# Last token block of an attention and MLP layer: one half of its output products made early instead of two

## The chip, the cores and the metric

The kernel runs on one core of a Trainium2 chip. The time is the device time of one execution in microseconds (us), the median of three runs. Inside the text, "at 1032.14" means 1032.14 us after the start of the profiled span, which is 1048.1 us long.

## What is computed

The reference is one transformer layer whose two branches are multiplied: self-attention with 32 heads of 32 on a normalised input, and an MLP with GELU, whose output goes through SiLU and gates the attention output. There are 2048 tokens of width 1024, in bf16.

```python
def reference(A_x, A_wqkv, A_wo, B_x, B_w1, B_b1, B_w2, B_b2):
    x  = A_x
    xn = _layernorm(x)
    s  = attention(xn, A_wqkv, A_wo)      # softmax(q k^T / sqrt(32)) v, 32 heads, then @ wo
    g  = _silu(gelu(_layernorm(xn) @ B_w1 + B_b1) @ B_w2 + B_b2)
    return x + s * g
```

The change touches only the last line of this: the product with `wo`, the multiplication by the gate `g`, and the addition of `x`.

## The kernel before: the parts that matter

The heads are worked through in 8 groups (`HG = 8`) of 4 heads, and within a group the queries in 8 blocks of 256 tokens (`qb`, `NQB = 8`). Attention of one block needs 8 "units"; each unit is one set of 8 score matmuls (TensorE, `L1176`), two exponentials of 128x1024 (ScalarE, `L1190`), and products with V and with ones (TensorE, `L730`). Everything else (projections, MLP, output products) is TensorE work that is laid between the score matmuls.

Who does what when is decided before the kernel runs, in Python. Every operation is recorded with an assumed duration, and a planner (`_Plan.run`) plays the five engines against each other and fixes for each engine one order of instructions. On the chip each engine runs its list in that order and waits on semaphores where the data demand it.

The output products come in the last head group. A `wo_item` is one 128-token half (`t2`) of a block and one 512-column half (`nh`) of the output: 8 matmuls of 128x512 that add up in one PSUM bank, one for each head group. Seven of them use head groups whose attention was finished long before; the eighth uses `ot7`, the block's attention in the last head group.

```python
def wo_item(qb, t2, nh, lo, hi):
    tb = 2 * qb + t2
    ri, xr, gr, rt = res_of(qb, t2)               # buffers with x and g of these 128 tokens
    it = _Item("wo")
    it.last = lo > 0                              # such an item opens only after the last score matmul
    for hc in range(lo, hi):
        ...                                       # bank += OT[hc]^T @ wo[hc][:, 512 columns]   (L735)
    ...
    if hi < HG:                                   # the early part: head groups 0 to 6
        dve(pk = bank * 0.5 * gr)                 # L1333, f32 result
        dve(pk = pk + xr)                         # L1335, f32
    else:
        dve(gr = bank * 0.5 * gr)                 # L1337
        if lo == 0:                               # a whole item
            dve(xr = gr + xr)                     # L1340, bf16
        else:                                     # the rest of a split item: head group 7 alone
            last = lambda e: e.tensor_tensor(xr[:, sl], gr[:, sl], pk, op=ALU.add)   # L1342
            if t2 == 0:
                pool(last, ...)                   # GpSimd
            else:
                dve(last, ...)                    # VectorE
            dma(...)                              # L1347: this 128x512 quarter goes out
    plan.queues["wo"].append(it)

# ... for each block qb of the last head group, after its attention:
lastq = qb == NQB - 1
for t2 in range(2):
    if not lastq:
        wo_load(qb, t2)
    for nh in range(2):
        wo_item(qb, t2, nh, 7 if lastq else 0, 8)
    if not lastq:
        wo_store(qb, t2)                          # L1312: 128x1024 of the output goes out
if qb == PART:                                    # PART = 4
    for t2 in range(2):
        wo_load(NQB - 1, t2)
        for nh in range(2):
            wo_item(NQB - 1, t2, nh, 0, 7)        # the early part of the last block
```

So for blocks 0 to 6 all four items of a block are whole. Block 7 is split: its four items over head groups 0 to 6 (28 matmuls) stand in the queue after those of block 4, and what is left for the very end is four single matmuls, each with its own multiplication and addition, and four quarters of the output.

Of the kernel before, what the change touches and what calls it, by code (L numbers as in the profile page):

```python
# [37 lines left out]
DN = (2, 3, 4, 5, 6, 7, 8, 9, 10, 11, 12, 13, 14, 15)  # L38
EVD = ()
PART = 4  # L40
WLAT = 3300
TR0 = 7
NCUT = 2
# [8 lines left out]
XB = 5  # L52
XW = 9
WVT = 6
ENGS = ("PE", "ACT", "DVE", "POOL", "SP")


# [18 lines left out]
class _Plan:  # L76
# [54 lines left out]
    def run(self, total_units, dense_slack):  # L131
# [51 lines left out]
        def release(o, t):  # L183
            for u in o.users:
                u.left -= 1
                f = o.fin
                if u.eng == "PE" and o.eng == "PE":
                    f = o.start + o.occ
                if f > u.ready:
                    u.ready = f  # L190
                if u.left == 0:
                    became_ready(u, t)
# [80 lines left out]
        def pe_step(t):  # L273
# [86 lines left out]
                                break  # L360
            best = None
            paced = None
            for c in cands:
                if c[0] <= t:
                    if c[1] == 0 and heads["pro"] >= len(self.queues["pro"]) and \
                            state["done"] < dense_total * (self.units_of(state["s"]) - dense_slack) / total_units:
                        paced = c
                        continue
                    if best is None or c[1] < best[1]:
                        best = c  # L370
                else:
                    nxt = min(nxt, c[0])
# [188 lines left out]
def bass_recurrent_scan__mha_block__mixer_channel_mlp__prompt_kernel(  # L561
# [39 lines left out]
    with ExitStack() as st:  # L601
# [79 lines left out]
        def c_b16(n):  # L681
            return 75 + 0.52 * n
# [632 lines left out]
        def wo_item(qb, t2, nh, lo, hi):  # L1315

            tb = 2 * qb + t2
            ri, xr, gr, rt = res_of(qb, t2)
            it = _Item("wo")
            it.need = wo_dma[qb, t2]  # L1320
            it.last = lo > 0
            for hc in range(lo, hi):
                def fn(e, b, hc=hc):
                    o7 = OTr[:, hc, tb * 128:(tb + 1) * 128] if hc < 7 else ot7[:, tb * 128:(tb + 1) * 128]
                    return full(e, bank(b), o7, wo_sb[hc][:, nh * 512:(nh + 1) * 512], hc == lo, hc == hi - 1)
                chunk(it, fn, Q512, [("OTr", hc, tb // 4) if hc < 7 else ("OT7", qb), ("wo", hc)])
            sl = slice(nh * 512, (nh + 1) * 512)
            k = 2 * t2 + nh
            pk = part[:, k]
            pt = [("h", h0 + 2 * k), ("h", h0 + 2 * k + 1)]  # L1330
            g, x = [("gr", ri, nh)], [("xr", ri, nh)]
            if hi < HG:
                dve(lambda e: e.scalar_tensor_tensor(pk, bank(it.bank), 0.5, gr[:, sl], op0=ALU.mult, op1=ALU.mult),  # L1333
                    c_ps(512), g, pt, 0, it)
                dve(lambda e: e.tensor_tensor(pk, pk, xr[:, sl], op=ALU.add), c_f32(512), x + pt, pt, 2.4)  # L1335
            else:
                dve(lambda e: e.scalar_tensor_tensor(gr[:, sl], bank(it.bank), 0.5, gr[:, sl], op0=ALU.mult, op1=ALU.mult),  # L1337
                    c_ps(512), g, g, 0, it)
                if lo == 0:
                    dve(lambda e: e.tensor_tensor(xr[:, sl], gr[:, sl], xr[:, sl], op=ALU.add), c_b16(512), g + x, x, 1)  # L1340
                else:
                    last = lambda e: e.tensor_tensor(xr[:, sl], gr[:, sl], pk, op=ALU.add)  # L1342
                    if t2 == 0:
                        pool(last, 1100, g + pt, x, 1)
                    else:
                        dve(last, c_f32(512), g + pt, x, 1)
                    dma(f"os{ri}{nh}", lambda e: e.dma_start(out2[tb * 128:(tb + 1) * 128, sl], xr[:, sl]), 131072, x, [])  # L1347
            plan.queues["wo"].append(it)
# [9 lines left out]
        for w in range(HG):  # L1358
            if w + 1 < HG:
                proj(w + 1, w)  # L1360
            else:

                def over(toks):
                    ops = []
                    for t in toks:
                        for d in [plan.last_w.get(t)] + plan.readers.get(t, []):
                            if d is not None and d not in ops:
                                ops.append(d)
                    return ops
                dead7 = over([("K", 0, n) for n in range(NPR)])  # L1370
                for qt in range(4):
                    dead = over([("xnT", t, h) for t in range(4 * qt, 4 * qt + 4) for h in range(2)])
                    for hg in range(HG - 1):
                        dma(f"otl{hg}{qt}", lambda e, hg=hg, qt=qt: e.dma_start(OTr[:, hg, qt * 512:(qt + 1) * 512],
                                                                          o_d[hg, :, qt * 512:(qt + 1) * 512]), 131072,
                            [("o_d", hg, 2 * qt), ("o_d", hg, 2 * qt + 1)], [("OTr", hg, qt)], 5, dead)
                    for hc in (2 * qt, 2 * qt + 1):
                        wd = over([[("wqk", 0)], [("wqk", 1)], [("wqk", 2)], [("wv",)], [("wv",)], [("dg", 0), ("dg", 1), ("sbc",)],
                                   [("Q", 0, n) for n in range(NPR)], [("Q", 0, n) for n in range(NPR)]][hc])
                        dma(f"wo{hc}", lambda e, hc=hc: e.dma_start(wo_sb[hc], A_wo[hc * 128:(hc + 1) * 128, :]), 262144, [],  # L1380
                            [("wo", hc)], 5, wd)
            for qb in range(NQB):
                g = w * NQB + qb
                if g == 0:

                    two = [_Item("pv"), _Item("pv")]
                    for pv in two:
                        pv.exp_of = {}
                    xs = []
                    for pos, (i, kp) in enumerate([(0, 0), (0, 1), (1, 0), (1, 1)] + [(i, kp) for kp in range(2, NKP) for i in range(2)]):  # L1390
                        x, vc = unit(i * 8 + kp, two[i], pos)
                        xs.append(x)
                        two[i].chunks.append(vc)
                    for pv in two:
                        pv.trigger = xs[TR0]
                        plan.pv_queue.append(pv)
                if g < 2:
                    norm(g, two[g], ot_t[g][:], [("ot", g)])
                    dma(f"ot{g}", lambda e, g=g, qb=qb: e.dma_start(o_d[0, :, qb * 256:(qb + 1) * 256], ot_t[g][:]),
                        65536, [("ot", g)], [("o_d", 0, qb)])  # L1400
                    continue
                pv = _Item("pv")
                pv.exp_of = {}
                vcs, ocs = [], []
                for kp in range(NKP):
                    x, vc = unit(g * 8 + kp, pv)
                    exps[g * 8 + kp] = x
                    vcs.append(vc)
                    if kp % 4 == 3:
                        ocs += ones_four(g * 8 + kp - 3, pv)  # L1410
                if len(ocs) == 3:
                    pv.chunks = vcs[0:6] + ocs[0:1] + vcs[6:7] + ocs[1:2] + vcs[7:8] + ocs[2:3]
                else:
                    pv.chunks = [vcs[0:6] + ocs[0:1] + vcs[6:8] + ocs[1:2], vcs + ocs][OLAG]
                late.append((pv, g))
                plan.pv_queue.append(pv)
                i = g % 2
                if w < HG - 1:
                    norm(g, pv, ot_t[i][:], [("ot", i)])
                    dma(f"ot{i}", lambda e, w=w, qb=qb, i=i: e.dma_start(o_d[w, :, qb * 256:(qb + 1) * 256], ot_t[i][:]),  # L1420
                        65536, [("ot", i)], [("o_d", w, qb)])
                    continue
                norm(g, pv, ot7[:, qb * 256:(qb + 1) * 256], [("OT7", qb)], dead7)

                lastq = qb == NQB - 1
                for t2 in range(2):
                    if not lastq:
                        wo_load(qb, t2)
                    for nh in range(2):
                        wo_item(qb, t2, nh, 7 if lastq else 0, 8)  # L1430
                    if not lastq:
                        wo_store(qb, t2)
                if qb == PART:

                    for t2 in range(2):
                        wo_load(NQB - 1, t2)
                        for nh in range(2):
                            wo_item(NQB - 1, t2, nh, 0, 7)
# [63 lines left out]
```

The softmax here doesn't subtract the row's maximum and nothing guards it: scores larger than these inputs give would overflow.

## Time and profile before

| what | value |
|---|---|
| time, median of 3 runs | 1049.85 us (1048.47 to 1050.28) |
| profiled span | 1048.1 us |
| TensorE busy | 1024.4 us, 98% of the span |
| ScalarE busy | 1016.8 us, 97% |
| VectorE busy | 959.5 us, 92% |
| GpSimd busy | 14.8 us, 1% |
| DMA | 159.63 MB, mean 152 GB/s |
| granted TensorE clock in the profiled run | 0.999 |

Three of the engines are over 90% busy, so the page as a whole does not tell what a change at the end is worth. The last twenty microseconds have to be read by themselves, instruction by instruction: when the last exponential ends, when the last matmul of TensorE starts, what VectorE and GpSimd still have to do after it, and when the last transfers leave. The timeline gives these; in it "PE" is TensorE, "DVE" VectorE, "ACT" ScalarE, "POOL" GpSimd, and "SPq" the queue that issues transfers. In a row that stands for several instructions (xN) the duration runs from the start of the first to the end of the last.

### The profile page before, as it was taken

How to read it: one execution, taken by the hardware profiler on the slowest of the kernel's cores; microseconds unless marked ns; L12 is line 12 of the kernel's file. 1: busy time of each engine (PE TensorE's matmuls, PEld its weight loads, DVE VectorE, ACT ScalarE, POOL GpSimd, SP SyncE). 2: the span in 40 equal slices, each digit the busy share in tenths (PEclk: the TensorE clock that was granted, in tenths of full speed). 3: DMA queues.
4: the chain of work that ended last, by engine and by line, in shares of the span. 5: the costliest groups of instructions: out<-in, count | busy, mean ns of one | idle time of the engine just before them, and what ended most of it. 6: DMA issues, size and time to landing. Idle time of an engine off the chain costs nothing.

```text
span 1048.1 us, 32171 instructions
## 1 busy us (share of the span) xinstructions
PE 1024.4 (98%) x14338; PEld 637.1 (61%) x14338; DVE 959.5 (92%) x1452; ACT 1016.8 (97%) x1110; POOL 14.8 (1%) x28
## 2 busy tenths in 40 slices
PE   8999999999999999999999999999999999999997
PEld 5555566656666656656776566556665567664442
DVE  8579999999999989999999989999989999979897
ACT  6799999999999999999999999999999999999993
POOL 2200000000000000000000000000000000000000
PEclk9999999999999999999999999999999999999999
DMA  8943457534266357533465456533565687672431
GB/s 230 201 126 110 127 153 218 168 94 127 86 196 184 105 143 211 150 104 107 132 180 169 125 155 193 138 96 107 154 200 157 173 240 226 204 206 98 136 102 61
DMA packets 300259, 159.63 MB, mean 152 GB/s; under 512 B 38106, under 2 KB 291034, under 8 KB 300122
## 3 DMA queue, kind: packets, MB, share of 16 engines
q1 hardware_dynamic: 300122, 157.59, 53.5%
q8 instruction: 112, 1.84, 0.7%
q14 instruction: 25, 0.20, 0.1%
HBM read 142.35 MB, written 12.06 MB: 147 GB/s over the span
## 4 chain that ended last, share of the span: by engine, by line
ACT 83%; PE 12%; DVE 2%; DMA 2%; SPq 1%; issue 0%; DVEq 0%
ACT P L1190 77%; PE ps L735 7%; ACT ut L1051 5%; PE ps L730 2%; PE ps L1176 2%; ACT gw L1087 1%; DVE ut L906 1%; DMA hT<-in_A_x_dram 1%; DMA w2r<-in_B_w_dram 1%; DMA big<-gw 0%; SPq L749 0%; DVE gw L936 0%; DVE w1r L1337 0%; DVE V L806 0%; SPq L757 0%; DVE qk L834 0%
## 5 line engine op out<-in xcount | busy, mean ns | idle before, releaser
L1190 ACT ACTIVATE P<-ps 128x1024 bf16<-128x1024 f32 x1024 | 964.1, 1238 | 10.2 <-PE ps L1176 10.0
L1220 DVE TENSOR_TENSOR PA<-P 128x2048 bf16<-128x2048 bf16 x245 | 297.6, 1217 | 17.8 <-ACT P L1190 16.4
L735 PE MATMUL ps<-yT,w1r 128*128 128x256 bf16 x1792 | 232.7, 273 | 1.3 <-DVE nv L1273 0.7
L735 PE MATMUL ps<-w2r,hT 128*128 128x256 bf16 x1792 | 225.0, 273 | 3.2 <-DMA w2r<-in_B_w_dram 1.3
L735 PEld LDWEIGHTS ps<-yT,w1r 128*128 128x128 bf16 x1792 | 162.7, 98 | 57.3 <-issue 30.6
L735 PEld LDWEIGHTS ps<-w2r,hT 128*128 128x128 bf16 x1792 | 163.8, 98 | 52.2 <-issue 29.8
L730 PE MATMUL ps<-P,V 128*32 128x256 bf16 x4096 | 144.2, 274 | 1.2 <-DVE xb L1036 0.7
L1225 DVE TENSOR_TENSOR PA<-PA 128x1024 bf16<-128x1024 bf16 x201 | 135.4, 681 | 1.2
L735 PE MATMUL ps<-big,qk 128*128 128x512 bf16 (+2 forms) x568 | 132.8, 360 | 2.4 <-DMA big<-gw 0.9
L735 PE MATMUL ps<-qk,big 128*128 128x256 bf16 (+1 forms) x736 | 127.5, 306 | 0.4 <-ACT big L885 0.3
L730 PEld LDWEIGHTS ps<-P,V 128*32 128x32 bf16 x4096 | 97.2, 96 | 33.6 <-issue 22.8
L1176 PE MATMUL ps<-qk 32*128 32x256 bf16 x2048 | 107.9, 273 | 4.9 <-ACT P L1190 4.5
L1176 PE MATMUL ps<-QKT 32*128 32x256 bf16 x2048 | 101.7, 273 | 1.2 <-ACT P L1190 1.1
L735 PEld LDWEIGHTS ps<-qk,big 128*128 128x128 bf16 x736 | 64.5, 98 | 43.9 <-issue 19.4
L1036 DVE TENSOR_TENSOR xb<-ps,b1T 128x512 bf16<-128x512 f32 x112 | 76.4, 683 | 8.4 <-PE ps L735 7.1
L735 PEld LDWEIGHTS ps<-big,qk 128*128 128x128 bf16 x568 | 47.9, 98 | 53.0 <-issue 16.7
L1176 PEld LDWEIGHTS ps<-qk 32*128 32x128 bf16 x2048 | 32.1, 92 | 74.0 <-ACT P L1190 69.2
L1176 PEld LDWEIGHTS ps<-QKT 32*128 32x128 bf16 x2048 | 30.3, 92 | 70.5 <-ACT P L1190 67.2
L1051 ACT ACTIVATE ut<-ut 128x1024 f32<-128x1024 f32 x56 | 71.8, 1282 | 0.0
L1054 DVE SCALAR_TENSOR_TENSOR hT<-ut,xb 128x1024 bf16<-128x1024 f32 x56 | 67.8, 1211 | 1.3 <-ACT ut L1051 0.9
L1049 DVE SCALAR_TENSOR_TENSOR ut<-hT,xb 128x1024 f32<-128x1024 bf16 x56 | 67.9, 1214 | 0.0
L1270 DVE STREAM_TRANSPOSE nt<-ps 128x256 f32<-128x256 f32 x64 | 28.6, 446 | 22.7 <-PE ps L730 22.6
(84 smaller groups left out, 540.6 us busy)
## 6 DMA issues: line engine op xcount, KB each, us to landing
w1r<-in_B_w_dram SPq DMA_DIRECT2D x224, 256.0 KB, 3.4
w2r<-in_B_w_dram SPq DMA_DIRECT2D x128, 448.0 KB, 4.4
qk<-in_A_wqkv_dram SPq DMA_DIRECT2D x16, 256.0 KB, 3.1
g_scratch<-gw SPq DMA_DIRECT2D x32, 128.0 KB, 2.6
o_scratch<-ot SPq DMA_DIRECT2D x56, 64.0 KB, 2.9
big<-o_scratch SPq DMA_DIRECT2D x28, 128.0 KB, 3.3
hT<-in_A_x_dram SPq DMA_DIRECT2D x10, 256.0 KB, 4.9
qk<-in_A_wqkv_dram SPq DMA_DIRECT2D x4, 512.0 KB, 4.0
```

The costliest lines, as they stand in the source:

```text
L730: ins = e.matmul(dst(j), lhsT=lhsT(j), rhs=rhs(j), start=start, stop=stop, tile_position=(0, 32 * j), skip_group_check=True)
L735: return e.matmul(dst, lhsT=lhsT, rhs=rhs, start=start, stop=stop, skip_group_check=True)
L906: dve(lambda e, t=t, c=c: e.bn_stats(stats[:, t, c, :], xst[t][:, c * 512:(c + 1) * 512]), 600, [XS(t)], [("st", t, c)], 1)
L1036: dve(lambda e: e.tensor_tensor(xb_t[i2][:, p % 2].rearrange("p (k t) -> p k t", k=2), bank(it.bank).rearrange("p (k t) -> p k t", k=2), b ...
L1049: dve(lambda e, r=r: e.scalar_tensor_tensor(ut_t[i2][:, r], h[:, r], 1.0 / GA, xb[:, r], op0=ALU.add, op1=ALU.mult), c_f32(r.stop - r.star ...
L1051: act(lambda e: e.activation(ut_t[i2][:], ut_t[i2][:], ACT.Tanh, scale=GC * GA), c_acts(1024), [("ut", i2, 0), ("ut", i2, 1)], [("ut", i2, ...
L1054: dve(lambda e, r=r: e.scalar_tensor_tensor(h[:, r], ut_t[i2][:, r], 1.0, xb[:, r], op0=ALU.add, op1=ALU.mult), c_f32(r.stop - r.start), [ ...
L1176: ins = e.matmul(bank(b0[j], kk * 256, (kk + 1) * 256), lhsT=QKT[sl][32 * j:32 * j + 32, 1, kb * 128:(kb + 1) * 128], rhs=QKT[sl][32 * j:3 ...
L1190: x = act(lambda e, h=h: e.activation(P[pi][:, 2 * h:2 * h + 2].rearrange("p j k q -> p (j k q)"), ps[:, pr[h] * 1024:(pr[h] + 1) * 1024], ...
L1220: add2.append(dve(lambda e, p0=p0, a0=a0: e.tensor_tensor(PA_all[:, a0:a0 + 2].rearrange("p u j q -> p (u j) q"), P_all[:, p0:p0 + 2, :, 0 ...
L1225: add4.append(dve(lambda e, a0=a0: e.tensor_tensor(PA[a0], PA[a0], PA[a0 + 1], op=ALU.add), c_b16(1024), [("PA", a0 + 1)], [("PA", a0)], P ...
L1270: a = dve(lambda e: e.transpose(nt_t[i][:], bank(pv.bank, 256, 512)), 368, [], [("nt", i)], 1, pv)
```

## The change

Only the first half (`t2 = 0`) of block 7 is still split. The second half is no longer made in part early: its two items run whole, 8 matmuls each, as the last ones of the queue, and each of its two 512-column quarters goes out as soon as it is added up. Its additions are then those of a whole item (two bf16 inputs) in place of those with an f32 partial sum. Two planner settings come with it: `XPE`, which is zero and so adds nothing, and `LATE`, a rule that keeps TensorE from opening other work when a score matmul has been ready for longer than the planner's 5000 ns.

```diff
+LASTP = 1
+XPE = 0
+LATE = 5000
@@ planner: release
                 if u.eng == "PE" and o.eng == "PE":
                     f = o.start + o.occ
+                elif u.eng == "PE" and o.eng == "ACT":
+                    f += XPE
@@ planner: choice of TensorE's next instruction
+            hold = INF
+            if state["s"] < len(self.s_queue):
+                o = self.s_queue[state["s"]]
+                if o.left == 0 and o.ready > t and heads["pro"] >= len(self.queues["pro"]):
+                    hold = o.ready + LATE
             for c in cands:
                 if c[0] <= t:
+                    if t + c[2].occ + (100.0 if c[2].mode != state["mode"] else 0.0) > hold:
+                        nxt = min(nxt, hold - LATE)
+                        continue
@@ wo_item
                 if lo == 0:
                     dve(lambda e: e.tensor_tensor(xr[:, sl], gr[:, sl], xr[:, sl], op=ALU.add), c_b16(512), g + x, x, 1)
+                    if qb == NQB - 1:
+                        dma(f"os{ri}{nh}", lambda e: e.dma_start(out2[tb * 128:(tb + 1) * 128, sl], xr[:, sl]), 131072, x, [])
@@ last head group
                 for t2 in range(2):
-                    if not lastq:
+                    if not (lastq and t2 < LASTP):
                         wo_load(qb, t2)
                     for nh in range(2):
-                        wo_item(qb, t2, nh, 7 if lastq else 0, 8)
+                        wo_item(qb, t2, nh, 7 if lastq and t2 < LASTP else 0, 8)
                     if not lastq:
                         wo_store(qb, t2)
-                if qb == PART:
-                    for t2 in range(2):
+                if qb == PART and LASTP:
+                    for t2 in range(LASTP):
                         wo_load(NQB - 1, t2)
                         for nh in range(2):
                             wo_item(NQB - 1, t2, nh, 0, 7)
```

## The prediction

> **What bounds the kernel now.** I read the page first: ScalarE is 97% busy, TensorE 98%. A share of 98% can belong to a limiting engine or to one that is merely fed to fit, so the second view is the ScalarE timeline near the end. One row there holds the last 31 exponentials.
>
> ```profile
> PE 1024.4 (98%) x14338; PEld 637.1 (61%) x14338; DVE 959.5 (92%) x1452; ACT 1016.8 (97%) x1110; POOL 14.8 (1%) x28
> ...
> 1003.24 28.90 ACT L1190 ACTIVATE P<-ps 128x1024 bf16<-128x1024 f32 x31
> ```
>
> The reader is to see 31 exponentials in 28.90 us without a gap: 0.93 us each, and the last ends at 1003.24 + 28.90 = 1032.14. Until then ScalarE sets the pace, and TensorE's matmuls only have to fit between its demands. Third view: the chain of waits of the last 30 us, from the last product with P on.
>
> ```profile
> 1032.27 0.55 PE ps L730 x16
> 1032.82 7.68 PE ps L735 x35
> 1040.50 0.02 issue
> 1040.52 0.69 DVE V L1337
> 1041.21 2.39 DVE w1r L1337 x4
> 1043.61 0.84 DVE V L1340
> 1044.44 0.60 DVEq L1452
> 1045.05 0.60 DVE w1r L1342
> ```
>
> After the exponentials the path is 8 us of wide output matmuls on TensorE, then 5 us of VectorE, then the last store. Fourth view: the timeline of that end.
>
> ```profile
> 1040.11 1.24 PE L735 MATMUL ps<-qk 128*128 128x512 bf16 x5
> 1040.52 0.69 DVE L1337 SCALAR_TENSOR_TENSOR V<-ps,V 128x512 bf16<-128x512 f32 x1 [0.57 <-PE ps L735]
> 1041.13 2.48 DVE L1337 SCALAR_TENSOR_TENSOR w1r<-ps,w1r 128x512 bf16<-128x512 f32 x4
> 1041.89 2.27 POOL L1342 TENSOR_TENSOR w1r<-w1r,hT 128x512 bf16<-128x512 bf16 x2 [998.16 <-DVE w1r L1337]
> ...
> 1043.52 0.92 DVE L1340 TENSOR_TENSOR V<-V 128x512 bf16<-128x512 bf16 x1
> 1044.37 1.28 DVE L1342 TENSOR_TENSOR w1r<-w1r,hT 128x512 bf16<-128x512 bf16 x2
> ...
> 1044.85 1.42 SPq L1347 DMA_DIRECT2D out_dram<-w1r  x3
> ```
>
> TensorE issues five matmuls in a row, the last of block 6 and the four singles of block 7: five results in about 1 us. VectorE then needs 5 evacuations (L1337) and three additions. It ends at 1044.37 + 1.28 = 1045.65, and the span ends 2.45 us later with the last store.
>
> **What the Trainium skill says.** (1) *SBUF — State Buffer*, "Who interferes with whom": a VectorE instruction with two SBUF inputs contends with a GpSimd instruction that reads SBUF, and the later of the two blocks fully; one with at most one SBUF input and no two-port mode does not. The trace agrees: L1337, which reads one input from PSUM, keeps a pitch of 0.60 us beside GpSimd (1041.13 to 1041.89 and on), but the L1340 addition at 1043.52 takes 0.92 us where the others of its line take 0.42; it ends 0.28 us after GpSimd's last one (1041.89 + 2.27 = 1044.16). (2) *VectorE: DVE Perf Modes*, "The perf-mode tier table": a two-tensor operation runs at double rate for bf16 in SBUF, at single rate for f32. Agrees: L1340 0.42 us, the f32 L1335 and L1342 0.68. (3) *TensorE: Matmul & The Clock Gate*, "Back-to-back issue gap": 512 columns cost about 216 ns alone and about 131 in a sustained stream of pairs. The trace has the first: rows of the timeline that begin an item's last matmul stand at 1034.93 and 1040.11, three items or 24 matmuls apart, 0.216 us each. (4) *DMA: Bandwidth & Descriptors*, "Anatomy of one DMA — SWDGE (gpsimd) path", puts the fixed cost of a transfer issued by GpSimd at about 2 us; here SyncE issues, and a 128 KB store lands in 1.7 to 2.0 us.
>
> **The change part by part.** The built order of instructions (no times in it) shows what the planner does. Setting `LASTP` to 2 in the changed file gives the old order on every engine, so `XPE` and `LATE` move nothing, and the first difference stands at TensorE instruction 14,000 of 14,324: only about the last 38 us differ. ScalarE's list is the same.
>
> *Removed early:* two items of 7 matmuls for block 7's second half: 14 x 0.216 = 3.0 us of TensorE, around 1013 to 1018, and on VectorE two L1333 and two L1335, 4 x 0.68 minus overlap, about 2.5 us. *Moved forward:* the matmuls of blocks 5 and 6 fill most of the hole. By count, the new order has 4 wide matmuls fewer before the last product with P (and 4 small ones with ones fewer, 0.1 us), and after it 43 instead of 39. So TensorE gets about 1.0 us of slack before the last exponential. ScalarE was gapless there, so I take **none** of it as gain: the last exponential stays at 1032.1.
>
> *TensorE's end:* the first of the 39 starts at 1032.76 (1040.11 minus 34 x 0.216), the last at 1040.97. With 43 the last starts at 1032.76 + 42 x 0.216 = 1041.83: **0.86 us later**.
>
> *VectorE's end:* the old order ends in a heap, the new one in an even row: block 6's last item, the two singles of block 7's first half, then the two whole items of 8. An evacuation starts 0.41 us after the item's last matmul starts (1040.11 to 1040.52), so results are ready at 1038.35, 1038.57, 1038.78, 1040.51 and 1042.24. VectorE works as follows. Three L1337 at a pitch of 0.60 to 0.65: 1038.35 to 1040.26. GpSimd's two additions of 1.155 us begin at 1039.73. The block 6 addition (two SBUF inputs) is blocked by the first until 1040.88 and ends near 1041.16. Then the first whole item's evacuation to 1041.85; its addition is blocked by GpSimd's second one to about 1042.3 and ends near 1042.6. Then the last evacuation 1042.55 to 1043.2 and the last addition, 0.42 us, to about 1043.65. That is **2.0 us earlier** than 1045.65. From the moment at which the last matmul can be evacuated (1041.38 before, 1042.24 after) 1.4 us of VectorE are left in place of 4.3.
>
> *Stores:* four quarters as before, but two now leave from VectorE at 1042.6 and 1043.65 instead of the three that follow each other from 1044.85. The final leg of 2.45 us stays or shrinks by a tenth. No load is added: block 7's x and g are fetched into the same buffers at the same places of the queue.
>
> Sum: +0.86 us on TensorE, -2.9 us between its last result and the last addition, 0 on ScalarE: about -2.0 us. 1049.85 - 2.0 = **1047.9 us**.
>
> **Rivals.** *TensorE is the bound before 1032 as well.* For: 98% busy, and the chain up to 1022 is all PE. Then the slack of 1.0 us would bring the last exponential forward, and the gain would be 3.0 us (1046.9). Against: the gapless ScalarE row. *GpSimd's lock takes it back.* If GpSimd's second addition starts before VectorE's waiting one, block 6's addition ends only near 1042.3, everything behind it slips by some 0.75 us, and the gain is 1.2 us (1048.6). For: both GpSimd additions are ready by then; against: in the old order VectorE lost only one such wait. *A score matmul comes late.* TensorE runs in order; with the new mix a product waiting for VectorE's sums (P added for the ones products) could hold up a score matmul and open a gap on ScalarE. By the old durations VectorE has those sums by about 1020.2 and TensorE asks at 1020.95, so I give it little weight, but each us of gap would be lost one for one, and two would cancel the gain. *The end was hidden:* if the last store set the end whatever VectorE does, nothing would change; against it, the last store is issued 0.2 us after the last addition.
>
> **Range and chances.** The central sum is -2.0, the rivals reach from -3.0 to 0. The three runs of before spread over 1.8 us, so the median itself is worth some 0.7 us either way. I put eight chances in ten on 1046.2 to 1049.4. Two per cent are 21 us, more than the part of the kernel that changes its order could plausibly give or lose: same 0.98, the rest split.
>
> **What would show it.** In the changed kernel's timeline: the last exponential ends at 1032.1 within 0.3 us (else the first or third rival); the last wide matmul starts near 1041.8; a whole item's L1350 follows it by 0.41 us or by what GpSimd makes of it; the last addition is a bf16 L1353 of 0.42 us and ends near 1043.6; one L1353 of 0.6 to 1.8 us stands beside GpSimd; the span ends about 1046.1. The prediction is wrong if ScalarE shows a gap after 1003, or if GpSimd's additions delay the last evacuation by more than a microsecond.

## The result, and the profile after

The changed kernel's first four runs gave a median of 1045.73 us (1045.19 to 1046.94) against 1049.88 us for the kernel before, a ratio of 0.9964 with a 95% interval of 0.9947 to 0.9982: 4.15 us faster where 2.0 were forecast, and 0.5 us under the forecast range. The interval is wide, 1.9 to 5.6 us. Two later comparisons with more runs gave 0.9979 (0.9972 to 0.9987; 16 runs against 38) and 0.9975 (0.9965 to 0.9984; 9 against 20), that is 2.2 and 2.6 us. All of this lies far under the two per cent (21 us) of which the prediction speaks.

The profiled spans differ by more: 1048.1 us before, 1043.5 after. So the first thing to find out is at which places of the span the 4.6 us lie. The page of the changed kernel shows the same shares as before, with only a few operations fewer:

```profile
span 1043.5 us, 32159 instructions
PE 1024.8 (98%) x14334; PEld 637.1 (61%) x14334; DVE 956.7 (92%) x1449; ACT 1016.5 (97%) x1110; POOL 15.6 (1%) x28
```

The last exponential is a good place to cut the span in two. ScalarE's timeline has one row for the last 86 of them, here of the kernel before and then of the changed kernel (start, duration, what):

```profile
952.77 79.37 ACT L1190 ACTIVATE P<-ps 128x1024 bf16<-128x1024 f32 x86
```

```profile
950.84 79.07 ACT L1203 ACTIVATE P<-ps 128x1024 bf16<-128x1024 f32 x86
```

They end at 1032.14 and at 1029.91. From there to the end of the span it is 15.99 us before and 13.58 us after. So 2.4 us of the difference lie behind the last exponential, 0.3 us in the 86 exponentials (79.37 against 79.07), and 1.9 us before the first of them, where the lists of instructions are the same in both kernels (in the traces the first instruction that differs is a weight load of TensorE at 1013.9). The end of the changed kernel, from its timeline:

```profile
1035.71 0.81 PE L748 MATMUL ps<-qk 128*128 128x512 bf16 x3
1036.13 0.69 DVE L1350 SCALAR_TENSOR_TENSOR V<-ps,V 128x512 bf16<-128x512 f32 x1 [0.58 <-PE ps L748]
...
1036.73 1.28 DVE L1350 SCALAR_TENSOR_TENSOR w1r<-ps,w1r 128x512 bf16<-128x512 f32 x2
1037.49 2.46 POOL L1357 TENSOR_TENSOR w1r<-w1r,hT 128x512 bf16<-128x512 bf16 x2 [994.57 <-DVE w1r L1350]
...
1037.93 1.00 DVE L1353 TENSOR_TENSOR V<-V 128x512 bf16<-128x512 bf16 x1
...
1038.86 0.68 DVE L1350 SCALAR_TENSOR_TENSOR w1r<-ps,w1r 128x512 bf16<-128x512 f32 x1
...
1039.57 0.67 DVE L1353 TENSOR_TENSOR w1r<-w1r 128x512 bf16<-128x512 bf16 x1
1039.60 0.38 PE L748 MATMUL ps<-qk 128*128 128x512 bf16 x1
1040.16 0.68 DVE L1350 SCALAR_TENSOR_TENSOR w1r<-ps,w1r 128x512 bf16<-128x512 f32 x1
...
1040.87 0.42 DVE L1353 TENSOR_TENSOR w1r<-w1r 128x512 bf16<-128x512 bf16 x1
1041.32 0.33 SPq L1355 DMA_DIRECT2D out_dram<-w1r  x1
```

The heap, five results within about 1 us, is gone. TensorE's last wide matmul (128x512) now starts alone, at 1039.60; it closes the second of two whole items, which follow the two singles (what is left of the split items) at a spacing of 1.73 us. Behind it VectorE has one evacuation (the instruction that takes an item's sum out of PSUM) and one bf16 addition to do, and then one store leaves; before there were four evacuations and three additions.

### The profile page after: what moved, and what is told of

It reads as the page before. It is cut to its first block, busy times and chain, and to the rows that moved or that the text cites. A ratio compares the mean times of both kernels' runs of the same rounds, so it can differ in the third digit from the quotient of the medians.

```text
span 1043.5 us, 32159 instructions
## 1 busy us (share of the span) xinstructions
PE 1024.8 (98%) x14334; PEld 637.1 (61%) x14334; DVE 956.7 (92%) x1449; ACT 1016.5 (97%) x1110; POOL 15.6 (1%) x28
## 4 chain that ended last, share of the span: by engine, by line
ACT 93%; PE 5%; DVE 1%; DMA 1%; issue 0%; POOL 0%; POOLq 0%
ACT P L1203 86%; ACT ut L1064 5%; PE ps L748 3%; ACT gw L1100 1%; PE ps L743 1%; PE ps L1189 1%; DVE ut L919 1%; DMA big<-gw 0%; DMA hT<-in_A_x_dram 0%; DVE w1r L1350 0%; POOL lnp L930 0%; PE ps L887 0%; DVE w1r L1353 0%; ACT big L898 0%; DVE V L1353 0%
```

## Experiments

In every table and paragraph "the end stretch" is the time from the end of the last exponential to the end of the span, read from each run's own trace.

### Both kernels again: how much is chance?

Both kernels were run again without an edit.

> The kernel before, unchanged. The two profiles differ by 4.6 us, of which 2.4 us lie after the last exponential (1032.1 to the end before, 1029.9 to the end after: 16.0 against 13.6 us) and 2.2 us before it. Theory A (the change acts on the end alone; most of what lies before the last exponential is chance: a first load 0.8 us later, one weight load that came late at 925): the ratio is 1.000, the stretch after the last exponential is again 16.0 us within 0.2, and the moment at which the last exponential ends differs from run to run by 1 to 2 us. Theory B (the change also speeds up what lies before): the last exponential ends again at 1032.1 within 0.4, with the same late weight load at 925.

> The changed kernel, unchanged. Theory A: the gain is 2.4 us of the end and about 0.3 us of two small gaps between exponentials that it closes, so a ratio of 0.9974 within 0.001 (2.0 to 3.5 us); the stretch after the last exponential is 13.6 us within 0.2; the last exponential ends anywhere from 1029.5 to 1032. Theory B: a ratio of 0.996 (over 3.7 us) and the last exponential at 1029.9 within 0.4 again.

> The changed kernel again, beside the one above on the same chip: 13.58 us after the last exponential, ratio to before 0.9975 within 0.001 (theory A), or 0.996 if what the first four runs showed was the change's own work (theory B).

| kernel, profiled run | last exponential ends | end stretch | ratio to before, 95% interval |
|---|---|---|---|
| before | 1032.14 | 15.99 | |
| before, again | 1030.51 | 15.99 | 0.9999 (0.9991 to 1.0007) |
| changed | 1029.91 | 13.58 | 0.9964 (0.9947 to 0.9982) |
| changed, again | 1030.03 | 13.58 | 0.9979 (0.9972 to 0.9987) |
| changed, third | 1031.35 | 13.58 | 0.9975 (0.9965 to 0.9984) |

The end stretch repeats to a few nanoseconds; the moment at which the last exponential ends moves by 1.4 to 1.6 us between runs of one and the same kernel. The views of waits name three sources. First the wait of ScalarE for the first rows of x (us in total, times, longest): before, before again, changed, changed again:

```profile
ACT yT L897 <- DMA hT<-in_A_x_dram: 3.7, 1, 3.7
```

```profile
ACT yT L897 <- DMA hT<-in_A_x_dram: 4.0, 1, 4.0
```

```profile
ACT yT L910 <- DMA hT<-in_A_x_dram: 2.8, 1, 2.8
```

```profile
ACT yT L910 <- DMA hT<-in_A_x_dram: 3.1, 1, 3.1
```

In the third run of the changed kernel it is 3.9 us. The second is a wait of TensorE, in the first 60 us, for transfers into `big`: 0.9 us in the kernel before and 0.5 in its repeat, 0.9 in the changed kernel, none of note in its second run, and in its third:

```profile
PE ps L748 <- DMA big<-gw: 1.6, 2, 0.8
```

These two work before 70 us; at 919 us the runs are as far apart as at 70 us, to within 0.02 us. The same exponential (number 906 of 1024) starts at 919.38 in the kernel before and at 918.87 in its repeat, and at 918.57, 917.99 and 920.01 in the three runs of the changed kernel. So all of the 1.4 us between the first and the third run of the changed kernel, and 0.5 of the 1.6 us between the two of the kernel before, come from the start.

The third source is a wait of TensorE for a block of MLP weights near 925, here in the kernel before and then in the changed kernel's second run:

```profile
PE ps L735 <- DMA w2r<-in_B_w_dram: 1.3, 1, 1.3
```

```profile
PE ps L748 <- DMA w2r<-in_B_w_dram: 0.9, 1, 0.9
```

The repeat of the kernel before has no such wait, nor have the changed kernel's first and third run. It comes and goes in both kernels, so it is not the change's work. Where it comes, ScalarE stands still for 1.0 us (before) or 0.6 us (changed, again). Theory B falls: the kernel before reached its last exponential at 1030.51 and not at 1032.1, and the changed kernel once at 1031.35. What is left of the 4.6 us as the change's own is 2.41 us in the end stretch and 0.3 us in the exponentials: 2.7 us, within the intervals of all three comparisons.

### The heap alone: all of block 7 early, its singles moved

```diff
 # before.py, after all items are queued
+wq = plan.queues["wo"]
+wq[-8:] = wq[-8:-7] + wq[-4:] + wq[-7:-4]    # block 6: first item, then block 7's four singles, then block 6's other three
```

> The kernel before with both halves of block 7 still made early (its 28 early matmuls stay), but its four single matmuls are moved in the queue from the very end to behind the first item of block 6, so that the last things on TensorE are three whole items. If the heap of evacuations and additions at the end is what the change removed (theory A), this alone removes it too, and without the 4 matmuls more: last wide matmul starts 8.8 us after the last exponential as before, last evacuation 0.4 us later, last addition ends near 10.8, end at 13.0 us after the last exponential in place of 16.0; ratio 0.997. If instead the early part itself is what costs (rival: the matmuls, f32 additions and loads around 1013 to 1018), the stretch stays over 15 us and the ratio within 0.001 of 1.

Measured: end stretch 13.11 us, ratio 0.9972 (0.9961 to 0.9982). The 28 early matmuls and the f32 partial sums are all still there, and yet the end is 2.9 us shorter than before. Its timeline:

```profile
1039.62 0.38 PE L735 MATMUL ps<-qk 128*128 128x512 bf16 x1
1040.06 0.68 DVE L1337 SCALAR_TENSOR_TENSOR V<-ps,V 128x512 bf16<-128x512 f32 x1
1040.66 0.75 DVE L1340 TENSOR_TENSOR V<-V 128x512 bf16<-128x512 bf16 x2
1041.43 0.33 SPq L1312 DMA_DIRECT2D out_dram<-V  x1
```

The last exponential of this run ended at 1030.78, so the last wide matmul starts 8.84 us after it, as in the kernel before (1040.97 - 1032.14 = 8.83). All of the gain lies between that matmul and the end. The heap alone accounts for it; the early work need not change. By the profiles this order takes 2.9 us off the kernel before, while the change takes 2.4 us off the end and 0.3 off the exponentials; the timed runs do not tell the two apart (0.9972 beside 0.9979 and 0.9975). What the early work costs is the next question.

### The early slots filled again with unused work

```diff
 # after.py
-if not (lastq and t2 < LASTP):  wo_load(qb, t2)
+if not lastq:                   wo_load(qb, t2)
 ...
-for t2 in range(LASTP):         # early part of block 7: load, two items of 7 matmuls
+for t2 in range(2):
```

The two items of the second half still run whole at the end, so the second half's early sums are computed and never read.

> The changed kernel, with the early part of block 7's second half computed as before, though nothing uses it (14 matmuls, 4 operations of VectorE, the loads at their old place); the whole items at the end stay. By the accounting of the prediction the freed early slots took up 10 matmuls of blocks 5 and 6. With the slots filled again, 53 wide matmuls stand after the last product with P in place of 43: the end comes 10 x 0.216 = 2.2 us later than in the changed kernel, 15.8 us after the last exponential, and the two small gaps between exponentials come back (0.3 us): ratio to before about 1.000. If the early slots were free anyway, the stretch stays at 13.6 us.

Measured: end stretch 15.75 us, ratio 0.9999 (0.9991 to 1.0007). The last matmul starts at 1043.26, 11.85 us after the last exponential (1031.41); in the changed kernel it is 9.69. That is 2.16 us, just 10 matmuls of 0.216. The exponentials lose their 0.3 us again; the row of the last 86 in ScalarE's timeline is as long as in the kernel before:

```profile
1043.26 0.38 PE L748 MATMUL ps<-qk 128*128 128x512 bf16 x1
...
952.04 79.37 ACT L1203 ACTIVATE P<-ps 128x1024 bf16<-128x1024 f32 x86
```

So the freed early slots are worth 2.2 us at the end, because other matmuls move up into them, and 0.3 us of small gaps between exponentials.

### Nothing of block 7 early

```diff
-LASTP = 1
+LASTP = 0
```

> The changed kernel with nothing of block 7 made early (LASTP 0): four whole items of block 7 at the end, no f32 partial sums, no GpSimd. Theory A: 48 wide matmuls stand after the last product with P (43 in the changed kernel), so the last one starts 5 x 0.216 = 1.1 us later, about 10.8 us after the last exponential; nothing holds VectorE, so the last evacuation follows by 0.41 us and the end comes 14.5 us after the last exponential (16.0 before, 13.6 changed). The two small gaps between exponentials stay closed (0.4 us). Together 1.9 us under before: ratio 0.998. If GpSimd and the f32 additions were what cost, this kernel would beat the changed one.

Measured: end stretch 14.77 us (forecast 14.5), ratio 0.9985 (0.9977 to 0.9992).

```profile
1042.50 0.38 PE L748 MATMUL ps<-qk 128*128 128x512 bf16 x1
1042.92 0.69 DVE L1350 SCALAR_TENSOR_TENSOR w1r<-ps,w1r 128x512 bf16<-128x512 f32 x1 [0.58 <-PE ps L748]
1043.64 0.42 DVE L1353 TENSOR_TENSOR w1r<-w1r 128x512 bf16<-128x512 bf16 x1
```

VectorE waits 0.58 us for TensorE before its last evacuation: the end is now set by TensorE alone, and the last matmul starts 11.01 us after the last exponential (1031.49), 1.3 us later than in the changed kernel. Of these 1.1 are the five matmuls more. The other 0.2 us lie before the first of them: the last product with P (P holds the exponentials) starts 0.30 us after the last exponential, in place of 0.06 in the changed kernel (1029.97), because one wide matmul stands in front of it.

```profile
1031.47 0.39 PE L748 MATMUL ps<-qk 128*128 128x512 bf16 x1
1031.79 0.40 PE L743 MATMUL ps<-P,V 128*32 128x256 bf16 x8
```

By the end stretch, one half made early is better than none and than two in the old order.

### GpSimd's part

```diff
 # nopool: after.py, L1357
-if t2 == 0: pool(last, ...)
-else:       dve(last, ...)
+dve(last, ...)
 # after_mid: after.py, after all items are queued
+wq = plan.queues["wo"]
+wq[-8:] = wq[-8:-5] + wq[-4:-2] + wq[-5:-4] + wq[-2:]    # the two singles before block 6's last item
```

> The changed kernel with the two last additions of block 7's first half on VectorE in place of GpSimd. In the changed kernel two additions of VectorE stand beside GpSimd and take 1.00 and 0.67 us instead of 0.42. If that wait is on the path that sets the end (rival), the stretch after the last exponential falls from 13.58 to 13.3 us or less. Theory A: the last evacuation waits mostly for its matmul, and VectorE gets 2 x 0.60 us of additions instead, so the stretch is 13.75 within 0.2.

> The changed kernel with the two singles of block 7's first half moved in front of block 6's last item, so that GpSimd's two additions are over before the last two items come. In the changed kernel the last evacuation starts 0.15 us after its matmul allows, held up by VectorE's waits for GpSimd. Theory A: those 0.15 us go, the stretch after the last exponential is 13.43 within 0.1. If GpSimd cost more than that on the path (rival), it is under 13.2.

Measured, from one profile each: 13.84 us without GpSimd, 13.46 us with the singles one item earlier, against 13.58; both as theory A has it. Without GpSimd, VectorE's list of evacuations and additions runs without a break into the last matmul's result:

```profile
1040.54 0.38 PE L748 MATMUL ps<-qk 128*128 128x512 bf16 x1
1041.01 0.68 DVE L1350 SCALAR_TENSOR_TENSOR w1r<-ps,w1r 128x512 bf16<-128x512 f32 x1
1041.61 0.75 DVE L1353 TENSOR_TENSOR w1r<-w1r 128x512 bf16<-128x512 bf16 x2
```

Both of the last two additions are left to the end there. So the wait for GpSimd is real (1.00 and 0.67 us for additions that take 0.42 without it) but costs no more than about 0.12 us on the path; taking GpSimd away costs 0.26, of which 0.14 lie behind the last addition (2.34 us to the end in place of 2.20).

### The last stores

```diff
 # one_store: after.py; block 7's second half in one 256 KB store
-                    if qb == NQB - 1: dma(... 128x512 quarter ...)
-                    if not lastq:                   wo_store(qb, t2)
+                    if not (lastq and t2 < LASTP):  wo_store(qb, t2)
 # spread_q: the kernel with spread singles; block 6's second half in two 128 KB stores
+                    if qb == NQB - 2 and t2 == 1: dma(... 128x512 quarter ...)
```

> The changed kernel with block 7's second half going out as one 256 KB store when both quarters are added up, in place of two of 128 KB. From the last addition to the end it is 2.20 us with a last store of 128 KB (changed kernel) and 2.48 us with one of 256 KB (the kernel with spread singles): the stretch after the last exponential becomes 13.58 + 0.28 = 13.85 us within 0.1. If the size of the last store does not matter (rival: only the time to land counts), it stays at 13.58.

> The kernel with spread singles, and the second half of block 6, which now ends the kernel, going out in two 128 KB quarters. The stretch after the last exponential goes from 13.11 to 12.83 us within 0.1, the two small gaps between exponentials stay as before: 3.15 us under before, ratio 0.997. This would be 0.3 us better than the changed kernel.

Measured: one store 13.89 us (from one profile), as forecast: the quarters are worth 0.3 us. But in the other kernel quarters made the end longer, 13.36 us in place of 13.11, a miss (ratio 0.9973, 0.9962 to 0.9983; the runs do not tell the two apart, the end stretches do). Its last additions and stores:

```profile
1041.55 0.75 DVE L1340 TENSOR_TENSOR V<-V 128x512 bf16<-128x512 bf16 x2
1041.98 0.81 SPq L1342 DMA_DIRECT2D out_dram<-V  x2
```

The two additions come one behind the other, so the two stores are issued in a row, and the span ends 2.73 us after the last addition (1042.30 to 1045.03). In the changed kernel, where the store before was issued 0.68 us earlier, it is 2.20. A quarter helps when it can leave early; it did not here. Two stores in a row do not explain the whole of it: the kernel without GpSimd issues its last two in the same way and ends 2.34 us after its last addition (1042.36 to 1044.70). What makes up the other 0.4 us stays open.

### A version built from this

```diff
 # after.py: three quarters of block 7 early, the last one whole
-wo_item(qb, t2, nh, 7 if lastq and t2 < LASTP else 0, 8)
+wo_item(qb, t2, nh, 7 if lastq and 2 * t2 + nh < 3 else 0, 8)
-for t2 in range(LASTP):  ...  for nh in range(2):
+for t2 in range(2):      ...  for nh in range(2 - t2):
+wq = plan.queues["wo"]
+wq[-8:] = wq[-8:-6] + wq[-4:-1] + wq[-6:-4] + wq[-1:]    # singles behind block 6's second item, whole quarter last
```

> Built from what the experiments showed: three of block 7's four quarters are made early and only the last runs whole, and their three singles stand in the middle, behind the second item of block 6. After the last product with P 38 wide matmuls stand (39 before, 43 in the changed kernel), and the last thing is one whole item with a 128 KB store. If the end is made of the wide matmuls plus what VectorE still has to do after the last of them (theory A): last matmul starts 0.61 + 37 x 0.216 = 8.6 us after the last exponential, evacuation 0.41 later, 1.15 us of VectorE, 2.2 us for the store: 12.4 us in place of 13.6 in the changed kernel. If the small gaps between exponentials come back (0.4 us), the net gain over the changed kernel is 0.8 us, else 1.2. Ratio to before 0.9965. If early work costs as much as it saves (rival), it is no faster than the changed kernel.

Measured: end stretch 12.61 us (forecast 12.4), 0.97 less than in the changed kernel; ratio 0.9967 (0.9956 to 0.9978), median 1045.60 us beside 1046.72 for the changed kernel's third comparison. The price shows in ScalarE's timeline, where the gapless row breaks:

```profile
952.65 68.07 ACT L1203 ACTIVATE P<-ps 128x1024 bf16<-128x1024 f32 x74
1021.09 11.11 ACT L1203 ACTIVATE P<-ps 128x1024 bf16<-128x1024 f32 x12 [0.37 <-PE ps L743]
```

```profile
1020.31 0.40 PE L1189 MATMUL ps<-QKT 32*128 32x256 bf16 x8 [0.26 <-issue]
1020.64 0.40 PE L743 MATMUL ps<-PA,ones 128*32 128x256 bf16 x8
```

The 86 exponentials now take 79.55 us (952.65 to 1032.20), 0.48 more than in the changed kernel. The score matmuls in front of the exponential at 1021.09 ended at 1020.71, so it was not they that held it up: it began 0.05 us after the products of summed P with ones (`PA,ones`) that follow them, and its row names the line of these products. Why it waited for them is not shown. (The idle 0.26 us in front of the score matmuls is a matmul that the trace lacks: its weight load stands at 1019.98.) The end misses its forecast by 0.2 us because here too a wide matmul stands in front of the last product with P, which starts 0.28 us after the last exponential (1032.48). By the profiles the net gain over the changed kernel is about 0.5 us, where 0.8 were forecast with such a gap; the intervals of the two overlap, so the timing alone does not settle it.

## Why the prediction was right or wrong

*What sets the end* was right: ScalarE almost gapless to the last exponential, then wide matmuls, then VectorE, then a store. *TensorE's end*: forecast 0.86 us later; the last wide matmul started 9.69 us after the last exponential in place of 8.83, exactly that. *VectorE's end*: the last addition was forecast 11.51 us after the last exponential and ended at 11.38 (1041.29 - 1029.91), against 13.51 before. GpSimd's lock held VectorE's additions as described: the block 6 addition ended 9.02 us after the last exponential, as forecast (1041.16 - 1032.14), and the last evacuation waited 0.15 us for VectorE instead of 0.3. From the start of the last matmul to the end of the last addition it is 4.68 us before and 1.69 after.

*The rivals*: that TensorE is the bound before the last exponential as well came true in part: of its 1.0 us of slack, 0.3 were gained. GpSimd's lock taking the gain back did not come. No score matmul came late in this kernel; the three-quarter version lost 0.48 us at the place in question, though behind products and not behind a score matmul. The end was not hidden. The sign named first, the last exponential at 1032.1 within 0.3 us, was no usable sign: that moment moves by more than a microsecond between runs of one kernel.

Three terms of the sum were mis-sized. "I take **none** of it as gain" left out 0.3 us. The row of exponentials looked gapless because each of them, at a mean of 1.15 us in the last 86, as a rule starts before the one ahead of it has ended; but two spacings of 1.09 and 1.05 us stood in it near 1020 and 1022, where the mean is 0.92. Both of these exponentials start 0.05 us after a set of score matmuls has ended (1020.43 + 0.40 and 1022.40 + 0.40), and both delays are gone in the changed kernel. The final leg was allowed to shrink by a tenth, but the sum took it as unchanged: it shrank from 2.48 to 2.20 us. The last store no longer follows another at once, and runs in which it does took 2.34 and 2.73 us; that this is the reason was not tested by itself. And VectorE's end was 0.13 us better. With them the sum is 2.7 in place of 2.0, which would have put the time at 1047.15, inside the range.

The step that failed is the one on range and chances: "the median itself is worth some 0.7 us either way". It took the spread of three runs of one kernel as the whole of the chance. The start of the program and one weight load shift the profiled runs by 1.4 to 1.6 us, and with four runs on each side the difference came out at 4.15 us, of which some 1.5 (4.15 - 2.7) are not the change's. Both sides leaned so as to widen it: the first median of the kernel before, 1049.88, lies above those of the two later comparisons (1048.61 and 1049.48), the first median of the changed kernel, 1045.73, below its later ones (1046.05 and 1046.72). On the later comparisons the gain was 2.2 to 2.6 us. So it was the luck of the draw that put the result below the range, and not the mechanism; the error is a range too narrow for such a draw. Which of the first eight runs had which wait is not known, apart from the profiled ones.

## What to carry to other kernels

When one engine paces a kernel to its last work item, look at what stands between that item and the end, and order it so that results come to the next engine one at a time; the order was worth 2.9 us here, with the same work. Work made early is not free where the engine that does it is nearly full: 14 matmuls early displaced 10 others to the end. Judge a change of a few tenths of a per cent by a stretch of the trace that repeats, not by a median of few runs.

## What the runs showed of the hardware

- From the last addition to the end of the span it took 2.20 us with a 128 KB store that followed the one before by 0.68 us, 2.34 to 2.73 us with one issued in a row with others (2.48 in the kernel before, with three), and 2.5 us with one of 256 KB.
- GpSimd's two additions took 2.27 us before and 2.46 us in the changed kernel, where two VectorE additions fell between and beside them, while VectorE's took 1.00 and 0.67 us instead of 0.42: in this trace both sides gave.
- A row of ScalarE instructions without a gap in the timeline still held 0.3 us of small delays; the merged row hides them, its length shows them (79.37 against 79.07 us for 86).
